# Two groups of filler matmuls per K pair, placed ahead of TensorE's waits for V and for K

## The chip, the cores and the metric

The kernel runs on one core of one Trainium2 chip. The metric is device time in microseconds (us), the median of several executions; the span quoted from a profile is a little shorter (1269.2 us where the time was 1270.96). Engines are named as the profile names them: PE is TensorE (PEld its weight loads), DVE VectorE, ACT ScalarE, SP SyncE, which here issues the large DMA transfers. "Granted clock" is the TensorE clock that the profile records as granted, as a share of full speed; in all records it is either 0.5 or 1.0, and values between are averages over both. A burst of matmuls (one pair's matmuls of one kind, in a row) is called warm where it ran at full clock and cold where it ran wholly or partly at half. PSUM is the memory that PE's matmuls write to.

## The reference, cut to what matters

One token attends over a long cache, plus a small mixer and a gate that cost almost nothing:

```python
# Hq, Hkv, Sk, Dh = 16, 8, 65536, 256 ; all bf16
q = (x @ wq).reshape(1, 1, 16, 256)
scores = einsum("bhqd,bhkd->bhqk", q, k) * 256**-0.5     # two query heads share one K/V head
p = softmax(scores)
o = einsum("bhqk,bhkd->bhqd", p, v)
a = o.reshape(1, 1, 4096) @ wo
out = g * a + (1 - g) * b                                # b: token mixer, g: sigmoid gate
```

K and V are 268 MB each. Every byte is read once, for two query rows; the work per byte is small.

## The kernel before

The cache is cut into 32 "K pairs" (`NP = 32`, four for each of eight heads). One pair is two K transfers of 4 MB (into the two halves of `kring`) and one V transfer of 8 MB (into the single `vbuf`), all issued by SP to one queue:

```python
for j in range(NP):
    for a in range(2):
        if j >= 1:
            eng.wait_ge(sem_tr[NB - 1], BODY * (j - 1) + DC * (a + 1))  # PE has transposed that half
        eng.dma_start(kring[:, a]..., k_src(2 * j + a)).then_inc(sem_k[a], 16)
    ...
        eng.wait_ge(sem_pv, j)                                          # PE has read all of vbuf
    n1 = NV if j < NP - 1 else NLATE                                    # 128 tiles; 96 in the last pair
    eng.dma_start(vbuf[:, 0:n1, :]..., v_src(j, 0, n1)).then_inc(sem_v, 16)
    # last pair: the remaining 32 tiles follow in three pieces of 16, 12 and 4
```

PE works through a pair in this order: for eight chunks, transposes of K into the PSUM banks of `kst` (line 272) and scores (line 284); then the softmax denominators (line 302); then, after the wait for V, 128 matmuls of two probability columns with a V tile of 256 columns (line 310), the last of which tells SP that `vbuf` is free:

```python
def values(j, c0, u16):
    for r in range(BODY):
        ...
        pe.matmul(acc[:, DENC:SELC], ones_sq[:, :], pT[:, r, :], ...)          # L302
    def some(n0, n1):
        pe.wait_ge(sem_v, u16)
        for n in range(n0, n1):
            r, nt = divmod(n, NT)
            o = 32 * (n % 4)
            ins = pe.matmul(acc[o:o + REP, 0:DH], pT[:, r, 2 * nt:2 * nt + 2], vbuf[:, n, :], ...)  # L310
        return ins
    with pe.If(j < NP - 1):
        some(NLATE, NV)
    some(0, NLATE).then_inc(sem_pv, 1)
...
with nc.Fori(0, H, 1, ...) as g:
    with nc.Fori(0, PPH, 1, ...) as m:
        ...
        keys(c0, u16)            # waits for K
        values(j, c0, u16)       # waits for V
    ...                          # end of a head: clear, normalise, project
late_values(*pieces[0])          # last 32 V tiles, as their pieces land (L328)
...
```

The softmax here doesn't subtract the row's maximum and nothing guards it: scores larger than these inputs give would overflow.

## Time and profile before

| | before |
|---|---|
| time, median of the first 3 runs | 1270.86 us |
| DMA queue, share of 16 engines' span | 99.6% |
| moved | 544 MB, 429 GB/s over the span |
| PE / ACT / DVE busy | 74% / 42% / 32% |
| granted clock, mean | 0.84 |
| V transfer, issue to landing | 33.4 us (median of 31) |

The DMA queues of the kernel before (packets, MB, share of the time of all 16 engines):

```profile
q1 hardware_dynamic: 16856, 544.22, 99.6%
```

The chain of work that ended last, before, by engine and by line:

```profile
DMA 85%; PE 15%; issue 0%; ACTq 0%; DVE 0%; DVEq 0%
```

Its pieces in order of time (start, length, what), two periods of it, without the 0.04 us of "issue" ahead of each burst:

```profile
677.62 5.76 PE acc L310 x119
683.40 34.14 DMA vbuf<-in_A_v_cache_dram
717.58 6.25 PE acc L310 x126
723.85 32.48 DMA vbuf<-in_A_v_cache_dram
```

Read alone, this is a loop of two links, V transfer and V matmuls, in which faster matmuls would shorten every period by their gain. The queue's share says otherwise. Of the 33.4 us that a V transfer "takes", its own 8.4 MB need about 19.4 us (an estimate, from the 432 GB/s that the trace shows between 52 and 1225 us); the other 14 us are, by that estimate, time in line behind K.

The costliest PE groups before (line, engine, operation, operands, count | busy us, mean ns of one | idle us before them and what ended it):

```profile
L272 PE MATMUL kst<-ident,kring 128*128 128x128 f32 x4096 | 554.6, 296 | 129.9 <-DMA kring<-in_A_k_cache_dram 120.3
L310 PE MATMUL acc<-vbuf,pT 128*2 128x256 bf16 x4064 | 179.5, 359 | 172.5 <-DMA vbuf<-in_A_v_cache_dram 172.5
```

PE idles 172 us waiting for V and 120 us waiting for K. In these waits the clock falls: ahead of 31 of the 32 V bursts it fell to half, and 30 of the 32 first bursts of transposes ran wholly or partly at half. Windows of two microseconds around one V wait of the kernel before (window; its length, PE, PEld, DVE, ACT and POOL busy us with their counts; granted clock, DMA share, GB/s):

```profile
673.00:675.00 2.00, 0.00 (x0) 0.00 (x0) 0.00 (x0) 0.00 (x0) 0.00 (x0) 1.00 0.91 395
675.00:677.00 2.00, 0.00 (x0) 0.00 (x0) 0.00 (x0) 0.00 (x0) 0.00 (x0) 0.52 0.71 276
677.00:679.00 2.00, 1.38 (x28) 0.92 (x32) 0.00 (x0) 0.00 (x0) 0.00 (x0) 0.50 1.22 509
679.00:681.00 2.00, 2.00 (x48) 1.24 (x40) 0.00 (x0) 0.00 (x0) 0.00 (x0) 0.50 0.91 393
```

PE went idle at 672.8, the clock halved about 675, and the V matmuls that start at 677.6 begin at half clock.

### The profile page before, as it was taken

Reading aid. Unit: us, or ns where it says so; the run is one execution under the profiler, and the core shown is the slowest. Engines: PE = TensorE matmul, PEld = TensorE weight load, DVE = VectorE, ACT = ScalarE, POOL = GpSimd, SP = SyncE. Lnnn points to the kernel's source line nnn. Section 1 sums busy time; section 2 is a strip of 40 time slices with the busy share of each in tenths; the row PEclk is TensorE's granted clock in tenths of the full one; section 3 lists DMA queues with packets and bytes.
Section 4 is the critical chain, followed back from the end, with each engine's and each line's share of the span. In section 5 each row is a group of like instructions: output and inputs, shape, how many; then the busy total and the mean of one; then the engine's idle time right before and its main releaser. Section 6 shows DMA issues by size and latency. Waiting matters only on the chain.

```text
span 1269.2 us, 37707 instructions
## 1 busy us (share of the span) xinstructions
PE 940.7 (74%) x17033; PEld 862.6 (68%) x17033; DVE 408.2 (32%) x672; ACT 535.5 (42%) x779; POOL 0.9 (0%) x7
## 2 busy tenths in 40 slices
PE   3788776878767787668776687866778666886768
PEld 3677665777657776567776677756678566876657
DVE  2454343443213332223322233322233222342223
ACT  1455433554334553335533355433455233553335
POOL 0000000000000000000000000000000000000000
PEclk9888787887878897888978789878888788897889
DMA  9999999999999999999999999999999999999997
GB/s 411 420 432 439 434 430 421 437 434 439 432 420 437 433 439 434 420 434 435 440 434 428 422 437 434 438 430 424 437 432 439 432 424 431 436 438 432 432 423 337
DMA packets 16879, 544.39 MB, mean 429 GB/s; under 512 B 1887, under 2 KB 3937, under 8 KB 4324
## 3 DMA queue, kind: packets, MB, share of 16 engines
q1 hardware_dynamic: 16856, 544.22, 99.6%
q8 instruction: 8, 0.13, 0.0%
q14 instruction: 3, 0.02, 0.0%
q10 hardware_dynamic: 12, 0.01, 0.0%
HBM read 544.22 MB, written 0.00 MB: 429 GB/s over the span
## 4 chain that ended last, share of the span: by engine, by line
DMA 85%; PE 15%; issue 0%; ACTq 0%; DVE 0%; DVEq 0%
DMA vbuf<-in_A_v_cache_dram 84%; PE acc L310 14%; DMA b_b<-in_B_b_dram 1%; PE sps L377 0%; PE sps L328 0%; PE sps L379 0%; DVE stat L457 0%; ACTq L581 0%; PE sps L335 0%; PE prj L348 0%; ACTq L585 0%; DVE out_g L576 0%; DVEq L456 0%; ACTq L584 0%; ACTq L583 0%
## 5 line engine op out<-in xcount | busy, mean ns | idle before, releaser
L605 ACT ACTIVATE ktT<-kst 128x1024 bf16<-128x1024 bf16 x512 | 499.4, 1021 | 677.6 <-PE kst L272 677.2
L272 PE MATMUL kst<-ident,kring 128*128 128x128 f32 x4096 | 554.6, 296 | 129.9 <-DMA kring<-in_A_k_cache_dram 120.3
L272 PEld LDWEIGHTS kst<-ident,kring 128*128 128x128 f32 x4096 | 505.3, 154 | 139.0 <-issue 138.5
L515 DVE COPY ktT<-kst 128x1024 bf16<-128x1024 bf16 x512 | 354.1, 692 | 737.1 <-PE kst L272 715.2
L310 PE MATMUL acc<-vbuf,pT 128*2 128x256 bf16 x4064 | 179.5, 359 | 172.5 <-DMA vbuf<-in_A_v_cache_dram 172.5
L310 PEld LDWEIGHTS acc<-vbuf,pT 128*2 128x2 bf16 x4064 | 116.4, 109 | 229.2 <-DMA vbuf<-in_A_v_cache_dram 175.6
L284 PEld LDWEIGHTS sps<-qcur,ktT 128*128 128x128 bf16 x8192 | 238.1, 96 | 3.3 <-issue 0.7
L284 PE MATMUL sps<-qcur,ktT 128*128 128x2 bf16 x8192 | 236.8, 163 | 0.6 <-issue 0.6
L596 ACT ACTIVATE pT<-sps 128x32 bf16<-128x32 f32 x256 | 51.8, 202 | 12.4 <-PE sps L284 12.4
L520 DVE COPY accs<-acc 128x288 f32<-128x288 f32 x8 | 3.7, 458 | 91.1 <-PE acc L310 91.1
L302 PE MATMUL acc<-pT,ones_sq 128*128 128x32 bf16 x256 | 16.5, 178 | 3.2
L611 ACT ACTIVATE z_b<-z_b 128x896 bf16<-128x896 bf16 x7 | 6.6, 949 | 20.9 <-DVE z_b L503 20.9
L302 PEld LDWEIGHTS acc<-pT,ones_sq 128*128 128x128 bf16 x256 | 10.9, 96 | 6.4 <-ACT pT L596 6.4
L365 PE MATMUL acc<-ones_sq,gu 1*128 1x1 bf16 x42 | 1.3, 161 | 8.6 <-DMA b_b<-in_B_b_dram 8.6
L365 PEld LDWEIGHTS acc<-ones_sq,gu 1*128 1x128 bf16 x42 | 1.2, 99 | 8.7 <-DMA b_b<-in_B_b_dram 8.7
L340 PE MATMUL acc<-zrow,ones_sq 1*128 1x292 bf16 x9 | 2.7, 305 | 4.7 <-DVE accs L520 4.0
L340 PEld LDWEIGHTS acc<-zrow,ones_sq 1*128 1x128 bf16 x9 | 0.9, 97 | 7.4 <-DVE accs L520 6.1
L348 PE MATMUL prj<-wo_sb,oTn 128*1 128x112 bf16 x128 | 2.9, 211 | 3.2 <-DVE oTn L531 3.2
L508 DVE TENSOR_TENSOR gu<-wtmp,z_b 128x896 bf16 x7 | 4.4, 625 | 1.2 <-issue 1.2
L497 DVE TENSOR_TENSOR z_b<-wtmp,u_b 128x896 bf16<-128x896 bf16 x7 | 4.4, 626 | 0.5
L501 DVE TENSOR_TENSOR z_b<-u_b,wtmp 128x896 bf16<-128x896 bf16 x7 | 4.4, 625 | 0.5
L495 DVE TENSOR_TENSOR wtmp<-u_b 128x896 bf16<-128x896 bf16 x7 | 4.4, 625 | 0.5
(82 smaller groups left out, 73.5 us busy)
## 6 DMA issues: line engine op xcount, KB each, us to landing
kring<-in_A_k_cache_dram SPq DMA_DIRECT2D x64, 4096.0 KB, 27.5
vbuf<-in_A_v_cache_dram SPq DMA_DIRECT2D x1, 6144.0 KB, 29.0
wo_sb<-in_A_wo_dram SPq DMA_DIRECT2D x8, 448.0 KB, 32.2
vbuf<-in_A_wq_dram SPq DMA_DIRECT2D x1, 3072.0 KB, 10.4
vbuf<-in_A_v_cache_dram SPq DMA_DIRECT2D x1, 1024.0 KB, 31.1
vbuf<-in_A_v_cache_dram SPq DMA_DIRECT2D x1, 768.0 KB, 32.5
vbuf<-in_A_wq_dram SPq DMA_DIRECT2D x1, 512.0 KB, 11.2
vbuf<-in_A_v_cache_dram SPq DMA_DIRECT2D x31, 33.4
```

The costliest lines, as they stand in the source:

```text
L272: ins = pe.transpose(kst[:, b, j * P:(j + 1) * P], kring_f[:, a, r * NT + 4 * b + j, :], ident[:, :])
L284: ins = pe.matmul(sps[:, par, 2 * nt:2 * nt + 2], ktT[:, par, b, ntl * DH + dj:(ntl + 1) * DH:2], qcur[:, dj, :], start=(dj == 0), stop=(d ...
L302: pe.matmul(acc[:, DENC:SELC], ones_sq[:, :], pT[:, r, :], start=False, stop=(r == BODY - 1), skip_group_check=True)
L310: ins = pe.matmul(acc[o:o + REP, 0:DH], pT[:, r, 2 * nt:2 * nt + 2], vbuf[:, n, :], start=False, stop=False, skip_group_check=True)
L495: vec.tensor_tensor(W, U, U, op=ALU.mult)
L497: vec.tensor_tensor(Z, W, U, op=ALU.mult)
L501: vec.tensor_tensor(Z, U, W, op=ALU.add)
L508: vec.tensor_tensor(gu[:, bass.ds(kt, MT), :], W, Z, op=ALU.mult).then_inc(s_pb, 1)
L515: vec.tensor_copy(ktT[:, k % KTB, b, :], kst_b[:, b, :]).then_inc(sem_ev[b], 1)
L596: act.activation(pT[:, k, :], sps[:, k % 2, 0:2 * NT], AF.Exp, scale=scale).then_inc(sem_exp, 1)
L605: act.activation(ktT[:, k % KTB, b, :], kst_b[:, b, :], AF.Copy).then_inc(sem_ev[b], 1)
L611: act.activation(z_b[:, :, :], z_b[:, :, :], AF.Tanh).then_inc(s_tanh, 1)
```

## The change

The intent is to keep PE busy in its two waits, so that the clock stays up and the matmuls after each wait run faster. The filler writes a PSUM bank whose content the next transposes overwrite; its sums are used by nothing.

```diff
+                spin(12)                                   # group 1: after the denominators, ahead of the wait for V
+
                 def some(n0, n1):
                     pe.wait_ge(sem_v, u16)
...
+            def spin(n):
+                for _ in range(n):
+                    pe.matmul(kst[:, NB - 1, :], ones_sq[:, :], ktT[:, KTB - 1, 0, 0:512], start=True, stop=True)
...
                     keys(c0, u16)
                     values(j, c0, u16)
+                    spin(12)                               # group 2: ahead of the wait for the next K
```

The lines below it move: the V matmuls become line 312, the late ones 330, the filler is line 397.

## The prediction

> **What bounds the kernel.** The DMA queue. The page gives it 99.6% of the 16 engines' span, 544 MB at 429 GB/s; PE has 74%, ACT 42%, DVE 32%. The chain that ended last is 84% V transfer and 14% V matmuls (line 310), as if the loop were bound by PE freeing the V buffer. It is not: a V transfer of 8.4 MB lands 33.4 us after its issue, but at 431 GB/s needs only 19.5 us; it sits about 14 us behind queued K. A K transfer lands after 27.5 us and needs 9.7. PE could free either buffer some 14 us later before the queue ran dry. V lands every 39.1 us (52.43 to 1225.44 us, 30 periods), the time of 16.8 MB at 429 GB/s.

> **What the change adds.** 24 matmuls of 512 columns per K pair, 768 in all. Nothing is removed, no transfer moves. [...]

> - Group 1 stands where PE waits for V: idle 4.9 us (672.8 to 677.6), 172.5 us in all. It fits.
> - Group 2 comes after the V matmuls have signalled, so it delays no V issue; it stands in the wait for K (5.3 us, 683.4 to 688.6). It fits, except at the seven head ends, where clear and projection come behind it and only 1.3 us of K wait is left[...].

> **What it is meant to gain.** The windows show the granted clock at 0.5 after each wait[...]. The first 32 transposes took 5.2 to 6.6 us against 3.9 later; 128 V matmuls took 4.9 to 6.4 us. [...] V matmuls should mostly run at full clock (about 3.4 us, estimated from a burst's last microsecond). [...] the transposes gain only sometimes. That is 2 to 3 us of PE time per pair, none of it on the path: V and K still land when the queue brings them.

> **Where it does show: the tail.** V's last 96 tiles start at 1259.46 and end 1263.5; late V matmuls and sums end 1265.9, the span 1269.2. [...] the 96 matmuls take about 2.6 us at full clock instead of 4.1[...] the 2.2 us of late matmuls follow: 1267.9, 2 us later. If warm transposes bring group 1 forward a microsecond, it is 1 us. The sum is +1 to +2 us.

> **Prediction.** 1272.5 us, range 1270.3 to 1276.0. Faster by over 2%: 0.01; within 2%: 0.97; slower by over 2%: 0.02.

> **What would show it.** Granted clock well above 0.84; V matmuls under 300 ns mean instead of 359; DMA share still over 99%, V period still 39.1 us; PE's waits for V and K down by about the groups' length; in the tail, twelve 512-column matmuls between line 310 and the late V matmuls, which end 1 to 2 us later relative to V's landing.

> **What would make it wrong.** A transfer rate that depends on what PE does (more PE reads slowing DMA writes, or issues coming at better times)[...]; a lower granted clock from more activity.

Cut from it, where marked, are a time for a filler matmul and delays of the clock that no trace or run of this case had shown when it was written, and what was worked out from them alone: how long a group takes, at full and at half clock, how much idle it leaves, when it ends, and how late transposes start at the head ends. Two terms of the tail's sum are the end of group 1 and the end of group 2. With them the sum came to 1267.9 us for the end of the late matmuls, against 1265.9 before: 2 us later, or 1 us where warm transposes bring group 1 forward. The group's length as measured is 2.75 us (below).

## The result

| | before | changed |
|---|---|---|
| median of 6 runs each | 1271.43 us (1270.54 to 1272.24) | 1271.99 us (1271.80 to 1272.37) |
| ratio | | 1.0005, 95% interval 0.9992 to 1.0018 |
| granted clock | 0.84 | 0.924 |
| PE busy | 940.7 us | 1067.7 us |
| DMA queue share | 99.6% | 99.5% |
| profiled span | 1269.2 us | 1270.4 us |

A ratio here is the mean time of one kernel's fast runs over that of the other's of the same rounds, so it is not quite the ratio of the quoted medians. The result is "same".

The lines of the changed kernel that answer to those of before: its queue, its chain by engine, and its PE groups:

```profile
q1 hardware_dynamic: 16856, 544.22, 99.5%
```

```profile
DMA 83%; PE 16%; issue 1%; SPq 0%; DVE 0%; ACT 0%; DVEq 0%
```

```profile
L272 PE MATMUL kst<-ident,kring 128*128 128x128 f32 x4096 | 523.3, 285 | 64.9 <-DMA kring<-in_A_k_cache_dram 55.4
L312 PE MATMUL acc<-vbuf,pT 128*2 128x256 bf16 x4064 | 166.7, 342 | 115.5 <-DMA vbuf<-in_A_v_cache_dram 115.5
L397 PE MATMUL kst<-ktT,ones_sq 128*128 128x512 bf16 x768 | 178.0, 382 | 0.0
```

The filler took 178 us of PE time, the two waits shrank by 57 and 65 us, transposes and V matmuls by 31 and 13 us. (A mean of 382 ns does not contradict a group of twelve in 2.75 us. Twelve times 382 ns would be 4.6 us, so their records overlap: within a group most start 215 or 216 ns apart.) The pieces of the chain, the answer to those shown before:

```profile
677.82 5.36 PE acc L312 x128
683.20 34.56 DMA vbuf<-in_A_v_cache_dram
```

V lands where it landed: 677.82 against 677.62 here. From the V burst near 92 us (92.34 before, 92.45 after) to the one near 1225 (1225.44, 1225.62), 29 periods, both kernels take 39.07 us per period.

The same V wait in windows, changed kernel:

```profile
673.00:675.00 2.00, 2.00 (x11) 0.90 (x10) 0.00 (x0) 0.00 (x0) 0.00 (x0) 1.00 0.91 393
675.00:677.00 2.00, 0.46 (x3) 0.00 (x0) 0.00 (x0) 0.00 (x0) 0.00 (x0) 1.00 0.71 279
677.00:679.00 2.00, 1.18 (x36) 0.90 (x40) 0.00 (x0) 0.00 (x0) 0.00 (x0) 0.85 1.18 491
679.00:681.00 2.00, 2.00 (x44) 1.36 (x40) 0.00 (x0) 0.00 (x0) 0.00 (x0) 0.50 0.91 393
```

Group 1 ended at 675.46. The clock did not fall in the wait; it fell soon after it, inside the V burst, after only 2.4 us of idle. The burst took 5.33 us, hardly better than the 5.73 of before.

```profile
674.98:678.40 3.42, 1.06 (x27) 0.51 (x28) 0.00 (x0) 0.00 (x0) 0.00 (x0) 1.00 0.90 364
712.53:715.94 3.41, 1.75 (x9) 0.59 (x6) 0.00 (x0) 0.00 (x0) 0.00 (x0) 1.00 0.89 384
715.94:719.36 3.42, 1.56 (x60) 1.36 (x64) 0.00 (x0) 0.00 (x0) 0.00 (x0) 1.00 1.02 441
```

How busy PE was in the stretches that kept the clock doesn't come out sharply: counted over these two traces (from 60 us on), a stretch at full clock with PE busy under 30% was followed by half clock in all 46 cases, one with over 90% by full clock in all 377, and of the 111 between, 59 were followed by full clock and 52 by half.

The only part of the span where PE's order shows is the end. The timeline of PE in the last pair, before (start, length, operation, count [idle before]):

```profile
1259.46 4.08 PE L310 MATMUL acc<-vbuf,pT 128*2 128x256 bf16 x96 [1.44 <-DMA vbuf<-in_A_v_cache_dram]
1263.70 0.95 PE L328 MATMUL sps<-pT,vbuf 128*128 128x2 bf16 x32
1264.98 0.94 PE L328 MATMUL sps<-pT,vbuf 128*128 128x2 bf16 x32
```

And changed:

```profile
1256.81 2.75 PE L397 MATMUL kst<-ktT,ones_sq 128*128 128x512 bf16 x12
1259.64 2.79 PE L312 MATMUL acc<-vbuf,pT 128*2 128x256 bf16 x96
1262.37 2.76 PE L397 MATMUL kst<-ktT,ones_sq 128*128 128x512 bf16 x12
1264.97 0.94 PE L330 MATMUL sps<-pT,vbuf 128*128 128x2 bf16 x32
1266.24 0.94 PE L330 MATMUL sps<-pT,vbuf 128*128 128x2 bf16 x32
```

V came 0.2 us later, the 96 matmuls gained 1.3 us from the full clock, group 2 cost 2.8 us after them, and the late matmuls end 1.3 us later (1267.18 against 1265.92). (The three terms make 1.7; the other 0.4 us are the gap ahead of the late matmuls before, and the overlap of the modelled ends after.) That is the 1.2 us between the two spans.

### The profile page after: what moved, and what is told of

Same layout as the page of the kernel before. It is cut to its first block, busy times and chain, and to the rows that moved or that the text cites. A ratio compares the mean times of both kernels' runs of the same rounds, so it can differ in the third digit from the quotient of the medians.

```text
span 1270.4 us, 39243 instructions
## 1 busy us (share of the span) xinstructions
PE 1067.7 (84%) x17801; PEld 895.0 (70%) x17801; DVE 408.2 (32%) x672; ACT 532.2 (42%) x779; POOL 0.9 (0%) x7
## 3 DMA queue, kind: packets, MB, share of 16 engines
q1 hardware_dynamic: 16856, 544.22, 99.5%
## 4 chain that ended last, share of the span: by engine, by line
DMA 83%; PE 16%; issue 1%; SPq 0%; DVE 0%; ACT 0%; DVEq 0%
DMA vbuf<-in_A_v_cache_dram 82%; PE acc L312 13%; DMA kring<-in_A_k_cache_dram 2%; PE kst L272 1%; PE kst L397 1%; PE sps L284 1%; PE sps L330 0%; PE sps L337 0%; SPq L215 0%; PE prj L350 0%; SPq L213 0%; DVE out_g L584 0%; PE acc L302 0%; ACT pT L604 0%; DVE oTn L539 0%
## 5 line engine op out<-in xcount | busy, mean ns | idle before, releaser
L272 PE MATMUL kst<-ident,kring 128*128 128x128 f32 x4096 | 523.3, 285 | 64.9 <-DMA kring<-in_A_k_cache_dram 55.4
L272 PEld LDWEIGHTS kst<-ident,kring 128*128 128x128 f32 x4096 | 471.2, 147 | 81.5 <-issue 78.4
L312 PE MATMUL acc<-vbuf,pT 128*2 128x256 bf16 x4064 | 166.7, 342 | 115.5 <-DMA vbuf<-in_A_v_cache_dram 115.5
L397 PE MATMUL kst<-ktT,ones_sq 128*128 128x512 bf16 x768 | 178.0, 382 | 0.0
L397 PEld LDWEIGHTS kst<-ktT,ones_sq 128*128 128x128 bf16 x768 | 70.6, 98 | 84.0 <-issue 9.3
## 6 DMA issues: line engine op xcount, KB each, us to landing
vbuf<-in_A_v_cache_dram SPq DMA_DIRECT2D x1, 6144.0 KB, 27.5
```

The lines of the kernel that those rows point to most:

```text
L272: ins = pe.transpose(kst[:, b, j * P:(j + 1) * P], kring_f[:, a, r * NT + 4 * b + j, :], ident[:, :])
L397: pe.matmul(kst[:, NB - 1, :], ones_sq[:, :], ktT[:, KTB - 1, 0, 0:512], start=True, stop=True)
```

## The experiments

The theory: the DMA queue sets the pace of every pair but the last, PE has time to spare in each, and only the last pair shows. The main rival reads the chain literally: V matmuls are a link of the loop, so a warm clock gains there per pair, and the filler gives the gain back. All twelve runs passed the comparison with the reference, also those whose V data are wrong on purpose; the comparison is not sharp enough to see those, so it says nothing about them.

### 1. One V matmul in eight

```diff
-                    for n in range(n0, n1):
+                    for n in range(n0, n1, 8):
...
-                        o = 32 * (n % 4)
+                        o = 32 * (n // 8 % 4)
```

> Before with one V matmul in eight (wrong result on purpose): 16 instead of 128 per pair, so V is handed back about 5 us sooner in each pair; the V transfers are all there. Theory (the queue is never dry, V issue may come 14 us later or 5 sooner): V period still 39.1 us, time about 1268.5 us (1267 to 1270), less only by the 3 us of matmuls in the tail. Rival (the chain's 14% of V matmuls are on the path): 31 x 5 us less, about 1115 us.

Measured: 1270.06 us (1269.85 to 1270.11, 4 runs), before 1271.03 in the same rounds; ratio 0.9992 (0.9976 to 1.0009). PE's V bursts fell to about 1 us, and V was handed back 3.9 to 5.5 us sooner in each pair. The rival's 1115 us is out by 155 us. The freed time turned into waiting in line. The issues of V by SP (KB each, us to landing), 31 of them, before:

```profile
vbuf<-in_A_v_cache_dram SPq DMA_DIRECT2D x31, 33.4
```

and with one V matmul in eight:

```profile
vbuf<-in_A_v_cache_dram SPq DMA_DIRECT2D x31, 37.7
```

Each transfer is issued about 4.3 us earlier and takes 4.3 us longer. The V period is what it was, 39.07 us (92.44 to 1225.51 us, 29 periods). That is what a full queue looks like.

The time is 0.06 us over the upper end of the range and 1.6 us over its middle, and the trace says why: the tail has a floor. The last four V tiles landed at about 1264.4 (the third piece's issue at 1227.9 plus the 36.5 us it took to land), so the late matmuls, which ended at 1264.87, could not have ended much sooner, however early PE was.

### 2. Each group alone, and group 2 left out after the last pair

`g1_only` drops the line `spin(12)` of group 2; `g2_only` that of group 1. `both_not_last`:

```diff
                     values(j, c0, u16)
-                    spin(12)
+                    with pe.If(j < NP - 1):
+                        spin(12)
```

> Only the group ahead of the wait for V, in every pair. Theory (the DMA queue sets the pace, only the tail shows): V period unchanged at 39.1 us. In the last pair the transposes start cold, so the group runs from about 1258.0 to 1260.7 and ends 1.1 us after V landed; the 96 matmuls take 2.8 us at full clock; no group 2 follows. Time about 1271.3 us (1270.7 to 1271.8), 0.5 to 1 us under the changed kernel, level with before. Rival (V matmuls are on the loop: 14% of the chain; warm V matmuls gain per pair and group 2 gives it back): this kernel should be about 10 us faster than the changed one.

> Only the group ahead of the wait for K, in every pair, the last included. Theory: V period unchanged; only the tail pays, as group 2 (2.76 us) stands between the last V matmuls and the late ones, less what warm transposes bring. Time about 1272.7 us (1272.0 to 1273.5). Rival (on the loop): some 10 us slower than the group for V alone.

> Both groups, but group 2 left out after the last pair. Theory: the changed kernel's tail without the 2.76 us: group 1 ends as V lands, 96 matmuls in 2.8 us, then the late matmuls wait for the last pieces of V (DMA ends near 1263.4). oTn about 1264.8 instead of 1267.2; time about 1269.7 us (1269.2 to 1270.3): 2.2 us under the changed kernel, 1.6 under before. If the tail is not the cause of the difference, the time stays at 1272.

| | time, median of 5 | ratio to before (before 1270.61) | clock |
|---|---|---|---|
| group 1 alone | 1272.11 (1271.08 to 1272.84) | 1.0015 (1.0001 to 1.0028) | 0.894 |
| group 2 alone | 1273.69 (1273.36 to 1274.08) | 1.0025 (1.0011 to 1.0038) | 0.869 |
| both, no group 2 at the end | 1270.12 (1269.54 to 1270.28) | 0.9996 (0.9983 to 1.0010) | 0.932 |

The rival's 10 us between group 1 alone and both are not there. Taking away twelve matmuls, those after the last pair, out of 768, took 1.9 us off the changed kernel's 1271.99 (other rounds, so only roughly), and 2.4 us off its profiled span (1268.0 against 1270.4). The timeline of the last pair in that kernel:

```profile
1259.32 2.79 PE L312 MATMUL acc<-vbuf,pT 128*2 128x256 bf16 x96
1262.56 0.95 PE L330 MATMUL sps<-pT,vbuf 128*128 128x2 bf16 x32 [0.45 <-issue]
1263.84 0.94 PE L330 MATMUL sps<-pT,vbuf 128*128 128x2 bf16 x32
```

The late matmuls now end at 1264.78, close to the floor that experiment 1 found. With group 2 alone, the V matmuls of the last pair ran cold (4.39 us) and the group followed: the late matmuls end at 1268.51, and that kernel is the slowest of the four, the one whose cost over before is clearest. Its time missed the forecast by 0.2 us over the upper end (1273.69 against 1273.5).

`g1_only` missed its forecast by 0.8 us in its timed runs, while its profile (1271.08) fitted. It was run again:

> The kernel with group 1 alone, a second time, as its timed runs (1272.11) stood 1 us over its own profile's reading (1271.08) and 0.8 over the forecast. Tail theory, with this trace's group 1 ending about 1.1 us after V landed: 1271 to 1272, within 0.5 us of the kernel before of the same rounds. If the 1.5 us over before come again, something beside the tail as the first trace shows it costs time, and this trace should show V's last landing later than 1259.5 or the last pair's matmuls later than in the first trace.

Measured: 1271.09 us (1270.72 to 1272.08, 6 runs), before 1270.97; ratio 1.0002 (0.9988 to 1.0015). The 1.5 us did not come again. The second trace shows one thing that differs between executions of the same kernel: the first transposes of the last pair took 6.26 us where the first trace has 5.30, so group 1 began at 1259.04 instead of 1258.08 and everything behind it ended 0.9 us later. (Both are starts of the first record of the group in the trace, which has eleven of the twelve.) Whether that explains the first five timed runs can't be told, as only one execution of each was traced.

### 3. Filler in the last pair alone

```diff
+                with pe.If(j > NP - 2):
+                    spin(6)
+
                 def some(n0, n1):
```

> Before plus six matmuls ahead of the last wait for V, nothing in the other 31 pairs. Theory: everything that the groups can gain is in the last pair: six take 1.4 us, 1258.0 to 1259.4, just up to V's landing, the 96 matmuls run in 2.8 instead of 4.1 us, time about 1269.8 us (1269.3 to 1270.5), like the kernel with both groups but the last. If the warm clock of the other 31 pairs is worth something, it stays above that kernel.

Measured: 1270.49 us (1269.99 to 1271.16), before 1270.61; ratio 1.0000 (0.9987 to 1.0014). The miss is 0.7 us against the forecast; the trace has the first transposes at 6.14 us, so the first of the six that the trace holds (it has five) began at 1258.98, where 1258.0 was forecast, and the group held the V matmuls to 1260.15; they then ran in 2.79 us as forecast. It lies 0.4 us from the kernel with filler in all pairs, so the 31 other pairs' warm clock is worth less than these runs resolve.

### 4. 22 matmuls per group

`spin(22)` for both, group 2 not after the last pair.

> 22 instead of 12 per group (about 4.8 us each), group 2 not after the last pair, so almost no idle is left for the clock to fall in. The group of 12 failed to keep the V matmuls warm (most bursts 5 to 6.5 us instead of 3.7), as 2.4 to 4.9 us of idle followed it. Theory: with 22, granted clock about 0.98, V bursts 3.7 us and first transposes 3.8 us nearly everywhere, mean V matmul about 280 ns; 9.6 us per pair stays under the 13.9 that PE has to spare (39 less 25.0 in the run with a quarter of V), so V period still 39.1 us. In the last pair group 1 ends about 2 us after V landed: time about 1272 us (1270.8 to 1273), 2 us over the kernel with 12 and no last group. If warm matmuls were worth anything on the loop, or more PE work slowed the queue, it would differ by much more.

Measured: 1271.95 us (1271.65 to 1272.24, 4 runs), before 1271.73; ratio 1.0004 (0.9988 to 1.0019), clock 0.974. PE was busy 90% of the span. The V matmuls:

```profile
L312 PE MATMUL acc<-vbuf,pT 128*2 128x256 bf16 x4064 | 138.6, 303 | 59.7 <-DMA vbuf<-in_A_v_cache_dram 59.7
```

So 41 us of V matmul time were saved against before (179.5), the clock is nearly full, and the V period is 39.07 us as ever (92.35 to 1225.43 us), the time what it was. The forecast of 280 ns was too good: only 17 of 31 V bursts ran at full clock. About 2.5 us of idle were left ahead of a burst (59.7 us in 24 waits), and that was enough to lose the clock in 14 of the 24.

### 5. How much PE has to spare

`dose36` has `spin(36)` twice. `v_quarter` is the kernel before with a quarter of each V transfer, all PE work kept; `v_quarter_spin` the same cut of the changed kernel:

```diff
-                n1 = NV if j < NP - 1 else NLATE
+                n1 = NV // 4 if j < NP - 1 else NLATE
...
-    ... pT[:, r, 2 * nt:2 * nt + 2], vbuf[:, n, :], ...
+    ... pT[:, r, 2 * nt:2 * nt + 2], vbuf[:, n % (NV // 4), :], ...
```

> 36 per group: 72 x 0.22 = about 16 us of matmuls per pair. Theory: PE's work per pair without groups at full clock is about 27 us (first scores to last, 22.5, and V 3.7, and loop); with 16 us it is 42 to 43, over the 39.1 us that the DMA queue needs: now PE sets the pace, no idle is left, clock 1.0. Time 1271 + 31 x 3 to 4 = 1365 to 1400 us. If single issues could come 14 us later without cost for good (as the forecast has it), the time would stay near 1275.

> Before with a quarter of each V transfer (32 of 128 tiles, reused; wrong result on purpose): 10.5 MB per pair instead of 16.8, all PE work kept. DMA needs 24.3 us per pair, PE at full clock about 27. Theory: PE sets the pace, DMA share falls under 95%, no waits for data, clock near 1.0: about 31 x 27 + 60 = 900 us (860 to 930). It shows how fast PE would go if data were there.

> The changed kernel with the same quarter of V. Theory: where PE sets the pace the groups cost all they take: 31 x 5.5 = 170 us more than its partner, about 1070 us. Rival (the groups pay for themselves by the clock): no slower than its partner.

| | time (one run each, state unknown) | DMA share | clock | per pair |
|---|---|---|---|---|
| quarter of V | 876.35 us | 96.1% | 0.988 | 24.94 us |
| quarter of V, filler | 1022.09 us | 83.7% | 0.998 | 30.09 us |
| 36 per group | 1355.76 us | 94.9% | 0.997 | 40.45 us |

"Per pair" is the distance of two neighbouring V bursts within a head (for 36 per group, of two first transposes). Two V bursts of the kernel with a quarter of V, PE's timeline:

```profile
602.61 3.67 PE L310 MATMUL acc<-vbuf,pT 128*2 128x256 bf16 x128
627.55 3.66 PE L310 MATMUL acc<-vbuf,pT 128*2 128x256 bf16 x128
```

With data at hand, PE needs 24.94 us for a pair; its waits for V are 1.7 us in all, and its list of waits has none for K. (Five early pairs, with mixer work, take 25.4, and those across a head's end 28.2 or more.) Against the queue's 39.07 us it has 14.1 us to spare in most pairs. Where it has nothing to spare, the filler costs its whole length: 30.09 less 24.94 is 5.15 us for 24 matmuls, or 215 ns a matmul. The V bursts that answer to those, with filler:

```profile
606.57 3.67 PE L312 MATMUL acc<-vbuf,pT 128*2 128x256 bf16 x128
636.66 3.67 PE L312 MATMUL acc<-vbuf,pT 128*2 128x256 bf16 x128
```

In all it cost 146 us. In the five early pairs with mixer work it cost 4.7 us, and across the seven head ends between 0.5 and 6.2 us; why was not looked into. And the dose agrees: 72 x 215 ns = 15.5 us, which with 24.94 makes the 40.4 us per pair that the run with 36 shows. (That is only 1.4 us over the queue's 39.07. The rest of the 85 us that this run lost to before lies in the seven pairs across a head's end, which take 43.2 to 46.6 us, and in some 6 us each at the start and in the tail.) That run's chain of what ended last has changed hands:

```profile
PE 96%; issue 2%; DMA 2%; ACT 0%; DVE 0%; SPq 0%; DVEq 0%
```

The forecast of 900 us was 24 us too high, inside its range; that of 1365 to 1400 us missed by 9, as PE's pair was put at 27 us and is 25. The 1070 us were 48 too high for the same reason and because 24 matmuls cost 5.15 us or less and not 5.5. The rival, that the groups pay for themselves, is out by 146 us.

### 6. The spread of equal kernels, and the best version a second time

> The kernel before, as a run of its own, to see how far equal kernels differ between executions: 1270.9 us (1269.4 to 1272.4), ratio 1.000. No theory expects anything else.

> Both groups, but group 2 left out after the last pair, a second time, beside the kernel before on this chip. Theory: 1270.0 us (1269.4 to 1270.6), 0.5 to 1 us under before: the last pieces of V land at about 1263.4, and what hangs on them cannot start sooner.

Measured: before again 1270.96 us (1269.90 to 1272.14), ratio 0.9999; both groups but the last 1270.17 us (1269.93 to 1272.12), ratio 0.9993 (0.9979 to 1.0007), before 1271.73. Twice it lay under before, by 0.5 and 1.6 us of medians, and both intervals hold 1. It can't be called faster.

The second trace of the kernel before is worth a line, since its span is 1267.9 against 1269.2:

```profile
1259.37 2.79 PE L310 MATMUL acc<-vbuf,pT 128*2 128x256 bf16 x96 [0.44 <-DMA vbuf<-in_A_v_cache_dram]
```

V landed within 0.1 us of the first trace, but here the pair's first transposes took 6.17 instead of 5.17 us, so PE had only 0.44 us of idle left ahead of the last burst instead of 1.44, and the clock did not fall (1.00 in the windows from 1257 to 1263, 0.50 from 1259 to 1262 in the first trace). The burst took 2.79 instead of 4.08 us: 1.29 us, about the 1.2 us between the two spans. What the filler buys at the end, the kernel before got by luck in this one of its two traced executions.

## Why the prediction was right

The measured time lies in the range: 1271.99 measured, 1272.5 predicted, and "within 2%" held. The number alone proves little, as the kernel before, at 1271.43 in the same rounds, lies in that range too; the steps have to be looked at one by one.

- **The queue bounds the kernel, and PE may be 14 us later per pair.** Right. The V period is 39.07 us with no filler, with 12 and with 22 per group; one V matmul in eight moved nothing but the time in line (33.4 to 37.7 us), and PE's spare time, measured by taking data away, is 14.1 us in most pairs. The forecast had got the 14 us from one transfer's time in line, which need not be what a loop can bear in every turn; the run with 36 per group confirms it as a limit of the loop.
- **Group length.** Measured were 2.75 us in the timeline, and 215 ns a matmul where PE sets the pace.
- **Tail +1 to +2 us.** Right in the traces: late matmuls end 1.26 us later, and the term that stands above was near (96 matmuls at full clock 2.8 us, predicted 2.6); group 2 took 2.76. The warm transposes did bring group 1 forward, as the smaller of the two cases had it. The timed runs alone could not show this: the medians differ by 0.56 us and the interval holds 1. There is luck in it: the trace from which the forecast was made has a cold last burst. Against the second trace of the kernel before, where that burst was warm and the late matmuls end at 1264.70, the same changed trace is 2.5 us later.
- **"V matmuls should mostly run at full clock", "the transposes gain only sometimes".** This step failed, with the roles swapped. Of 31 V bursts 6 ran at full clock (0 before), mean 342 ns and not under 300; of 32 first bursts of transposes 18 did (1 before). Two things were missed. The faster transposes bring group 1 forward, so that the wait after it grew, up to 5.0 us, instead of staying as short as the forecast had it; it was 4.3 us or more ahead of 16 of the 31 bursts, and all of these ran cold. And 2.4 us of idle was already too much at one burst: the clock fell at 678.40, after PE had started again. The prediction had also given three delays, the shortest of 2.7 us, from PE's going idle to the clock's fall. In the trace of the kernel before, the clock fell 0.6 to 2.3 us after PE went idle ahead of every V burst but the first, so 2.3 us of idle or less sufficed for the fall there. Where a burst did run warm it took 3.66 us, for the 3.4 that were estimated. The step cost nothing in the time, because no matmul in those pairs is on the path.
- **"PE's waits for V and K down by about the groups' length."** Too much: 57 and 65 us, where 32 groups of 2.75 us are 88. Most of the rest, 44 us, went to PE having got ahead through warm transposes and V matmuls, and then waiting longer.

## What to carry to other kernels

When a chain shows a transfer and the matmuls that free its buffer in turn, look at the queue's share first. Here it was 99.6%: V issued 4.3 us earlier took 4.3 us longer to land (33.4 to 37.7 us), and what PE did between issues left the period at 39.07 us until its spare time of 14.1 us per pair was used up (40.45 us with 36 matmuls per group). Filler that kept the clock up (0.84 to 0.974 with 22 per group) was free in such waits and worthless there (ratio 1.0004); it counted at the end, where the last data land and PE's work is exposed (96 matmuls in 2.79 instead of 4.08 us), and there it must not stand behind the last data (group 2 cost 2.76 us). Measure the spare time by taking data away, and place filler right up to the end of a wait: at the beginning of a wait that is longer than the filler it held the clock here for only 6 of 31 bursts.
